# The operands of a second feed-forward layer: x on VectorE, two sums per round kept in DRAM, operands split four products ahead

## The chip, the cores and the metric

One core of a Trainium2 chip runs the whole program. The metric is the device time of one execution in microseconds (us). Engines are named as in the profile: PE is the matmul engine TensorE, PEld its weight loads, DVE is VectorE, ACT is ScalarE, POOL is GpSimd, SP is SyncE, whose queue issues nearly all transfers.

## What is computed

Pooled attention (4 batches, 8 heads, 576 tokens) gives a matrix x of 2304 tokens by 512. A gated layer of width 1536 follows, and then the layer in which the change lies (`_moe2_ref` of the reference, d_ff = 2048):

```python
h = x @ w_in
sp = np.where(h > 20.0, h, np.log1p(np.exp(np.minimum(h, 20.0))))
g = h * np.tanh(sp)
return (g @ w_out).astype(np.float32)
```

The nonlinearity is Mish. All inputs and outputs are float32.

## The kernel before

The 2304 tokens are worked in three **pairs** of two groups of 384 tokens (`NG = 384`, `p` = 0, 1, 2; "second pair" is p = 1, "last pair" is p = 2). Each float32 matmul is made of three matmuls of a rounded type: a tile is split into a high part (ACT casts it, L1197) and a low part (DVE subtracts the high part, L1201), and high*high, low*high and high*low are added up in PSUM.

Both products, x @ w_in and g @ w_out, are taken as 2x2 block products with seven block multiplications instead of eight (Winograd's form), in which sums of blocks are multiplied. So x, the weights and g are needed in sums, and those are split into high and low parts as well.

For the second and the last pair the work stands in two stages:

- **Rounds.** Eight rounds `i` = 0..7, each with seven products of x (`product(k)`, L122 to L124, 42 matmuls of 384 columns), one after the other on PE. DVE adds each product to a running sum (L1347), ACT applies Mish. A round leaves four blocks of g: `a`, `g2[2i]`, `g2[2i+1]` and `u`. From these two operands (`gu`, `gd`) go at once into the output accumulators `acc` (18 matmuls, in the next round). The weights of the next round come from DRAM in four transfers (`split_weights`, L1231).
- **Jobs.** Then 40 jobs of 9 matmuls of 256 columns each (`job`, L1289) add the other five output products: eight of kind 1 (operand `a_at[i]`), eight of kind 5 (operand S1 = `a_at[i]` + `g2[2i]`, L1496), eight of kind 6 (operand `g2[2i]`), eight of kind 7 (operand S3 = `g2[2i+1]` - `g2[2i]`, L1502), eight of kind 4 (operand `g2[2i+1]`). The order is written out: 1 x8, 5 x3, 6 x8, 5 x3, 7 x8, 5 x2, 4 x8; the last two run in the next pair's first round. Between jobs 2 and 4 stand the last round's two operands (18 matmuls to `acc`). The operand of job j+3 is split behind job j (`operand`), into one of four buffers `g`. DVE forms S1 in place behind the job of kind 1, and S3 behind the job of kind 6. The right-hand sides of the kinds 5, 6, 7 and 4 come from DRAM (`load_sum`, L1283), each into the place of one that is no longer used. `ob` is a pool of three buffers for output rows.

While the second pair's jobs run, the x of the last pair is made: `load_x2` (L146) brings four blocks for each half k of the depth, and `prep_x2_pool` makes 7 sums, each with a high part by ACT (L178) and a low part by POOL (L181), and 4 differences by POOL (L184). For the second pair the same is made by DVE in `prep_x2` (L157, L160), while the first pair's jobs run.

Every engine runs its instructions in the order in which they are written; SP too, so that a transfer that waits holds up all behind it.

Of the kernel before, what the change touches and what calls it, by code (L numbers as in the profile page):

```python
# [57 lines left out]
def tile_pooled_attention_moe_mish(  # L58
# [42 lines left out]
    w2od = [dram.tile([128, 512], F32, name=f"w2od{i}") for i in range(NF2)]  # L101
    wsd = [dram.tile([128, 2, 512], F32, name=f"wsd{i}") for i in range(NF)]
    wspd = [[dram.tile([128, 2, n], F32, name=f"wp{i}_{j}") for j, n in enumerate((512, 512, 512, 256))] for i in range(NFP)]
    td = [dram.tile([128, 4, 2, 256], F32, name=f"td{i}") for i in range(NFP)]

    def acc_tiles():
# [19 lines left out]
    with tc.manual_schedule():  # L126
# [42 lines left out]
                [lo(4, b21)],  # L169
            ]  # L170

        def prep_x2_pool(k, j):

            P, A = nc.gpsimd, nc.scalar
            b11, b12, b21, b22 = (st_t[r, c] for r, c in ((0, 0), (0, 1), (1, 0), (1, 1)))

            def hi(i, t):
                return lambda: A.copy(out=top[i, k][0], in_=t)  # L178

            def lo(i, t):  # L180
                return lambda: P.tensor_sub(out=top[i, k][1], in0=t, in1=f32(top[i, k][0]))  # L181

            def sub(out, a, b):
                return lambda: P.tensor_sub(out=out, in0=a, in1=b)  # L184

            return {
                j: [hi(1, b11), hi(3, b22), hi(2, b21), lo(1, b11), sub(b11, b12, b11), sub(b12, b22, b12)],
                j + 1: [lo(3, b22), sub(b22, b22, b11), lo(2, b21), sub(b21, b21, b22)],
                j + 5: [hi(5, b11)],
                j + 6: [hi(7, b12), lo(5, b11)],  # L190
                j + 7: [hi(6, b22), lo(7, b12)],
                j + 9: [hi(4, b21), lo(6, b22), lo(4, b21)],
            }

        def prep_w(ws, st):

# [975 lines left out]
        with ExitStack() as bctx:  # L1172
# [131 lines left out]
                        rhs = [w[:, b, half[h]] for b in range(2)]  # L1304
                        out_half(acc[t][0][:, half[h]], g, t, rhs, i + h == 0, i == NFP - 1)

            pend, after, keep = [], None, []
            g2 = {}
            for p in range(NPR):
                o = 2 * NG * p  # L1310
# [5 lines left out]
                for i in range(NFP):  # L1316
                    n = NFP * p + i
                    wt = w_sets[i % 2]
                    f1, f2 = 2 * i, 2 * i + 1
                    if p == 0:  # L1320
                        split_weights(i, True)
                        tt = load_rows_out(i)
                    if NFP <= n + 1 < NFP * NPR and i < NFP - 1:
                        split_weights((i + 1) % NFP, False)
                    if wino and 0 < i < 5:
                        for m in (2 * i - 2, 2 * i - 1):
                            load_sum(5, m)

                    a = a_at[i] if wino else a7
                    u = u0 if wino or i % 2 == 0 else a6  # L1330
                    if p == 0:
                        for f in (f1, f2):
                            g2[f] = late[f] if f in late else pb.tile([128, NG], F32, name=f"g2_{f}")

                    def product(k, *reads):

                        ps, home = bank(f"p{k}")
                        part, c0 = PART[k]
                        for kk in range(2):
                            xh, xl = top[k, kk]  # L1340
                            c = slice(c0 + 128 * kk, c0 + 128 * kk + 128)
                            mm3(ps[:, :NG], wt[part], c, xh, xl, kk == 0, kk == 1)
                        for out, in0 in reads:
                            if in0 is None:
                                nc.scalar.copy(out=out, in_=ps[:, :NG])
                            else:
                                nc.vector.tensor_add(out=out, in0=in0, in1=ps[:, :NG])  # L1347
                        banks.append(home)

                    product(1, (a, None))  # L1350
                    product(6, (u, a))
                    product(5, (v, u))
                    product(7, (g2[f2], v), (u, u))
                    nc.scalar.activation(out=g2[f2], in_=g2[f2], func=AF.Mish)  # L1354
                    if i == NFP - 1:
                        gs = {}
                        for f in range(2):
                            src = a_at[f] if wino else g2[f]
                            gs[f] = high(src, False)
                            low(src, gs[f])  # L1360
                        if wino:
                            g = gs[2] = w_sets[0][0][:, :, :NG]
                            A.copy(out=g[:, 0, :], in_=a_at[2])
                            low(a_at[2], g)
                    if p == 0 and i < NFP - 1:
                        run_all(prep_w(ws_of.pop(n + 1), w_sets[(i + 1) % 2]) if n else rows)
                    run_all([keep[:1]])
                    if n + 3 < NFP:
                        load_ws(n + 3)
                    run_all([pend])  # L1370
                    if after is not None:
                        after()
                    pend, after = [], None
                    if acc is None:
                        acc = [bank(f"acc{t}") for t in range(NTG)]
                    product(2, (a, a))
                    if wino:
                        A.activation(out=a, in_=a, func=AF.Mish)
                        product(3, (g2[f1], v))
                        A.activation(out=g2[f1], in_=g2[f1], func=AF.Mish)  # L1380
                        V.tensor_sub(out=v, in0=g2[f2], in1=a)
                        product(4, (u, u))
                        A.activation(out=u, in_=u, func=AF.Mish)
                        V.tensor_add(out=g2[f1], in0=g2[f1], in1=v)
                        V.tensor_sub(out=v, in0=u, in1=g2[f1])
                        gu, gd = high(u, False), high(v, False)
                        low(u, gu)
                        low(v, gd)
                        pend = [lambda i=i, acc=acc, gu=gu, gd=gd: out_pair(acc, i, gu, gd)]
# [56 lines left out]

                def operand(j):

                    if 2 < j <= last:
# [12 lines left out]

                more = {}
                if not final:
                    more = prep_x2_pool(0, 3)
# [10 lines left out]
                for j, (k, i) in enumerate(jobs[:-2]):  # L1476
# [7 lines left out]
                    if 8 <= j < 11 or 19 <= j < 22:  # L1484
                        t, h = (j - 8, 0) if j < 11 else (j - 19, 1)
                        x = ob[t][:, half[h]]
                        V.tensor_add(out=x, in0=x, in1=X[t][0][:, half[0]])
                        if h == 0:
                            leave(x, 128 * t, 0)
                    if j == 29:  # L1490
                        for t in range(NTG):
                            A.copy(out=c22[t], in_=X[t][0][:, half[0]])
                    if j < 2 or j > 3:
                        operand(j + 3)
                    if k == 1:
                        V.tensor_add(out=a_at[i], in0=a_at[i], in1=g2[2 * i])  # L1496
                        load_sum(6, i)
                    if k == 5:
                        load_sum(4, i)
                    if k == 6:  # L1500
                        load_sum(7, i)
                        V.tensor_sub(out=g2[2 * i], in0=g2[2 * i + 1], in1=g2[2 * i])  # L1502
                    if 4 <= j < 7:
                        t = j - 4
                        ob[t] = pb.tile([128, 512], F32, tag="ob", name="ob", bufs=3)
# [7 lines left out]
                        banks.append(Y[t][1])  # L1513
                    run_all([more.pop(j, [])])
                    if not final:
                        if j == 5:
                            split_weights(0, False)
                        if j == 17:
                            load_x2(p + 1, 1)
                            more = prep_x2_pool(1, 22)  # L1520
                if final:
                    for t in range(NTG):
                        for j in (last - 1, last):
# [49 lines left out]
```

## Time and profile before

| | us |
|---|---|
| three runs, lowest / median / highest | 869.18 / 869.37 / 870.87 |
| the profiled execution, its own time | 869.25 |
| its span, first to last instruction | 867.5 |
| PE busy / share of the span | 854.8 / 99% |
| DVE busy / share | 632.7 / 73% |
| ACT busy / share | 452.2 / 52% |
| POOL busy / share | 173.7 / 20% |

The table says which engine is filled over the whole span; a matmul's end is modelled, so a busy PE is not PE at its best rate. What a stage leaves unused is seen from the starts of matmuls: in undisturbed stretches they follow each other at a fixed distance.

### The profile page before, as it was taken

What the parts mean: (1) busy time and instruction counts of PE and PEld (TensorE: products, weight loads), DVE (VectorE), ACT (ScalarE), POOL (GpSimd) and SP (SyncE); (2) the same over time, 40 slices, a digit from 0 to 9 for tenths busy, and PEclk for the clock granted to TensorE, in tenths of its full rate; (3) what the DMA queues carried; (4) which work ended last, traced back from release to release, by engine and by line L of the source; (5) the groups of instructions that cost most, each with busy time, mean ns of one, the idle gap of its engine ahead of it and who ended that gap; (6) DMA issues with size and microseconds to landing.
All of it is one profiled execution on the core that took longest, in us unless ns stands there. A gap on an engine that the chain in (4) does not pass through costs nothing.

```text
span 867.5 us, 14376 instructions
## 1 busy us (share of the span) xinstructions
PE 854.8 (99%) x5044; PEld 782.1 (90%) x5044; DVE 632.7 (73%) x1160; ACT 452.2 (52%) x1083; POOL 173.7 (20%) x182
## 2 busy tenths in 40 slices
PE   8999999999999999999999999999999989999998
PEld 7878887888888888999999999998999979999998
DVE  6989764776675565878998877766666798667784
ACT  7655675555565554534545655555333455334454
POOL 3566430210210000001100045442000065000000
PEclk9999999999999999999999999999999999999999
DMA  9898527998788876256658789987577355777353
GB/s 344 305 315 266 176 79 241 283 274 252 243 263 265 226 222 218 97 201 229 237 198 294 271 297 336 325 307 251 195 258 255 115 198 168 245 244 225 125 189 100
DMA packets 113891, 202.30 MB, mean 233 GB/s; under 512 B 34588, under 2 KB 64284, under 8 KB 113820
## 3 DMA queue, kind: packets, MB, share of 16 engines
q1 hardware_dynamic: 112812, 199.40, 69.4%
q10 hardware_dynamic: 1008, 2.00, 0.7%
q8 instruction: 40, 0.66, 0.3%
q14 instruction: 31, 0.25, 0.1%
HBM read 141.44 MB, written 53.62 MB: 225 GB/s over the span
## 4 chain that ended last, share of the span: by engine, by line
PE 86%; DVE 5%; ACT 4%; DMA 2%; issue 1%; POOL 1%; SPq 0%; ACTq 0%; DVEq 0%
PE acc L1207 8%; PE x L1289 7%; PE p L124 7%; PE p L122 7%; PE p L123 7%; PE acc L122 4%; PE acc L123 4%; PE acc L124 4%; PE acc L1289 4%; PE q L123 3%; PE q L124 3%; PE q L122 3%; PE pv L593 3%; PE pv L594 3%; PE pv L597 3%; PE pg L593 3%
## 5 line engine op out<-in xcount | busy, mean ns | idle before, releaser
L122 PE MATMUL p<-top,w2s 128*128 128x384 f32 x216 | 72.4, 335 | 0.0
L124 PE MATMUL p<-top,w2s 128*128 128x384 f32 x216 | 72.4, 335 | 0.0
L123 PE MATMUL p<-top,w2s 128*128 128x384 f32 x216 | 72.4, 335 | 0.0
L1207 PE MATMUL acc<-w,g 128*128 128x512 f32 x288 | 67.1, 391 | 0.0
L1207 PEld LDWEIGHTS acc<-w,g 128*128 128x128 f32 x288 | 54.0, 188 | 10.9
L954 ACT CAST gh<-sg 128x512 fp32r<-128x512 f32 x36 | 22.3, 621 | 69.8 <-DVE sg L949 69.8
L122 PE MATMUL acc<-gh,wo 128*128 128x512 f32 x144 | 57.1, 397 | 0.0
L123 PE MATMUL acc<-gl,wo 128*128 128x512 f32 x144 | 56.4, 391 | 0.0
L124 PE MATMUL acc<-gh,wo 128*128 128x512 f32 x144 | 56.2, 390 | 0.0
L1201 DVE TENSOR_TENSOR g<-g,g 128x384 fp32r<-128x384 f32 x64 | 41.4, 662 | 19.0 <-ACT g L1197 18.7
L1197 ACT CAST g<-g 128x384 fp32r<-128x384 f32 x64 | 31.8, 512 | 30.4 <-PE x L1289 15.8
L456 ACT ACTIVATE e<-sc,mx 128x72 f32<-128x72 f32 x144 | 43.7, 333 | 3.1 <-DVE mx L444 3.0
L1085 POOL TENSOR_TENSOR g<-g,y 128x384 f32<-128x384 f32 x12 | 12.2, 1016 | 153.6 <-ACT g L1082 153.6
L122 PEld LDWEIGHTS p<-top,w2s 128*128 128x128 f32 x216 | 40.7, 188 | 0.3
L123 PEld LDWEIGHTS p<-top,w2s 128*128 128x128 f32 x216 | 40.7, 188 | 0.3
L124 PEld LDWEIGHTS p<-top,w2s 128*128 128x128 f32 x216 | 40.6, 188 | 0.0
L124 PE MATMUL p<-x1c,w2s 128*128 128x384 f32 x120 | 40.1, 335 | 0.0
L122 PE MATMUL p<-x1c,w2s 128*128 128x384 f32 x120 | 40.1, 334 | 0.0
L123 PE MATMUL p<-x1c,w2s 128*128 128x384 f32 x120 | 40.1, 334 | 0.0
L1289 PE MATMUL x<-w2s,g 128*128 128x256 f32 x288 | 38.4, 293 | 1.8 <-DVE g L1201 1.0
L1354 ACT ACTIVATE g<-g 128x384 f32<-128x384 f32 x24 | 12.6, 525 | 51.7 <-DVE g L1347 51.7
L1289 PEld LDWEIGHTS x<-w2s,g 128*128 128x128 f32 x288 | 36.7, 199 | 3.1 <-DVE g L1201 1.7
(324 smaller groups left out, 2538.0 us busy)
## 6 DMA issues: line engine op xcount, KB each, us to landing
w2s<-wp SPq DMA_DIRECT2D x48, 512.0 KB
wo<-wod SPq DMA_DIRECT2D x39, 512.0 KB
wp<-w2s SPq DMA_DIRECT2D x24, 512.0 KB
raw<-w2i SPq DMA_DIRECT2D x16, 512.0 KB
raw<-w2o SPq DMA_DIRECT2D x16, 512.0 KB
w<-td SPq DMA_DIRECT2D x32, 256.0 KB
w2s<-td SPq DMA_DIRECT2D x32, 256.0 KB
wr<-wv SPq DMA_DIRECT2D x12, 512.0 KB
```

The lines of the kernel that those rows point to most:

```text
L122: nc.tensor.matmul(ps, wt[:, 0, cols], xh, start=start, stop=False)
L123: nc.tensor.matmul(ps, wt[:, 0, cols], xl, start=False, stop=False)
L124: nc.tensor.matmul(ps, wt[:, 1, cols], xh, start=False, stop=stop)
L456: nc.scalar.activation(out=e_t[T][:, 4 * g + h, :], in_=s[:, h, :], func=AF.Exp, scale=-1.0, bias=mx_t[T][:, 4 * g + h, :], accum_out=sm_t ...
L593: nc.tensor.matmul(ps[:, c0:c1], w, xh[:, k, c0:c1], start=(k == 0), stop=False)
L594: nc.tensor.matmul(ps[:, c0:c1], w, xl[:, k, c0:c1], start=False, stop=False)
L597: nc.tensor.matmul(ps[:, c0:c1], w, xh[:, k, c0:c1], start=False, stop=(k == KD - 1))
L954: nc.scalar.copy(out=gh, in_=sg)
L1197: nc.scalar.copy(out=g[:, 0, :], in_=src)
L1201: nc.vector.tensor_sub(out=g[:, 1, :], in0=src, in1=f32(g[:, 0, :]))
L1207: nc.tensor.matmul(acc[t][0], g[:, a, c], w[:, b, :], start=(f == 0 and first), stop=(f == NF2 - 1 and last),)
L1289: nc.tensor.matmul(ps, g[:, a, c], rhs[b], start=start and a + b == 0, stop=stop and a == 1, skip_group_check=True)
```

## The change

1. The low parts and differences of the last pair's x move from POOL to DVE, spread over one job each (`prep_x2_slots` in the place of `prep_x2_pool`). The second half's blocks are loaded behind job 11 instead of job 17, and the weights of the last pair's first round behind job 23 instead of job 5.
2. In the rounds 0 to 5 of the second pair, S1 is formed as `g2[2i]` (before its last subtraction) + `g2[2i+1]`, and S3 one round later, each in a buffer of `ob`, and both are stored to DRAM (`sd`, 12 transfers of 192 KB). During the jobs they are loaded again over `a_at[m]` and `g2[2m]` (12 transfers). The sums of rounds 6 and 7 are formed among the jobs 13 to 16. In the last pair all sums stay with their jobs.
3. In both pairs the operands of jobs 0 to 4 are split before the jobs begin, the first three into the place of round 6's weights, and from then on an operand is split four jobs ahead. The additions of `ob` stand together behind jobs 8 and 19.

```diff
-        def prep_x2_pool(k, j):
+        def prep_x2_slots(k, j):
...
-                return lambda: P.tensor_sub(out=out, in0=a, in1=b)
-
-            return {
-                j: [hi(1, b11), hi(3, b22), hi(2, b21), lo(1, b11), sub(b11, b12, b11), sub(b12, b22, b12)],
-                j + 1: [lo(3, b22), sub(b22, b22, b11), lo(2, b21), sub(b21, b21, b22)],
...
+                return lambda: V.tensor_sub(out=out, in0=a, in1=b)
+
+            parts = [
+                [hi(1, b11)],
+                [lo(1, b11), hi(3, b22)],
+                [sub(b11, b12, b11)],
+                [sub(b12, b22, b12), hi(2, b21)],
+                [lo(3, b22), hi(5, b11)],
+                [sub(b22, b22, b11), hi(7, b12)],
+                [lo(2, b21)],
+                [sub(b21, b21, b22), hi(6, b22)],
+                [lo(5, b11)],
+                [lo(7, b12), hi(4, b21)],
+                [lo(6, b22)],
+                [lo(4, b21)],
+            ]
+            return {j + m: part for m, part in enumerate(parts)}
...
                     product(7, (g2[f2], v), (u, u))
                     nc.scalar.activation(out=g2[f2], in_=g2[f2], func=AF.Mish)
+                    run_all([late_sum])
+                    run_all([spill])
...
-                        V.tensor_add(out=g2[f1], in0=g2[f1], in1=v)
+                        if kept:
+                            sums = [pb.tile([128, 512], F32, tag="ob", name="sk", bufs=3)[:, :NG] for _ in range(2)]
+                            V.tensor_add(out=sums[0], in0=g2[f1], in1=g2[f2])
+                            V.tensor_sub(out=g2[f1], in0=sums[0], in1=a)
+                            spill = [
+                                lambda m=m, i=i, x=x: nc.sync.dma_start(out=sd[i][m], in_=x) for m, x in enumerate(sums)
+                            ]
+                        else:
+                            V.tensor_add(out=g2[f1], in0=g2[f1], in1=v)
...
+                        if kept:
+                            late_sum = [
+                                lambda x=sums[1], f1=f1, f2=f2: V.tensor_sub(out=x, in0=g2[f2], in1=g2[f1])
+                            ]
...
-                    if j < 2 or j > 3:
-                        operand(j + 3)
-                    if k == 1:
-                        V.tensor_add(out=a_at[i], in0=a_at[i], in1=g2[2 * i])
+                    if j > 2:
+                        operand(j + 4)
+                    if final:
+                        if k == 1:
+                            V.tensor_add(out=a_at[i], in0=a_at[i], in1=g2[2 * i])
+                        if k == 6:
+                            V.tensor_sub(out=g2[2 * i], in0=g2[2 * i + 1], in1=g2[2 * i])
+                    else:
+                        for m in {0: (0, 1, 2), 8: (3,), 9: (4,), 10: (5,)}.get(j, ()):
+                            nc.sync.dma_start(out=a_at[m], in_=sd[m][0])
+                        if 12 <= j < 18:
+                            nc.sync.dma_start(out=g2[2 * (j - 12)], in_=sd[j - 12][1])
...
-                        if j == 5:
+                        if j == 23:
                             split_weights(0, False)
-                        if j == 17:
+                        if j == 11:
                             load_x2(p + 1, 1)
-                            more = prep_x2_pool(1, 22)
+                            more = prep_x2_slots(1, 17)
```

How the change moves instructions is shown at three places. First VectorE among the second pair's jobs 5 to 10. `g` is an operand's low part, `aw`, `a6`, `a7` hold `a_at`, `st` a block of x and `top` its high and low parts, `ob` with `x0` to `x2` is an addition of output rows. Before:

```order
L1496 TENSOR_TENSOR a6_5248<-a6_5248,g2_12_5242 128x384
L1201 TENSOR_TENSOR g_7338<-aw_6422,g_7338 128x384
L1496 TENSOR_TENSOR a7_5249<-a7_5249,g2_14_5244 128x384
L1487 TENSOR_TENSOR ob_7287<-ob_7287,x0_7190 128x256
L1201 TENSOR_TENSOR g_7357<-g2_0_5257,g_7357 128x384
L1487 TENSOR_TENSOR ob_7307<-ob_7307,x1_7191 128x256
```

Now:

```order
L1209 TENSOR_TENSOR g_7345<-aw_6437,g_7345 128x384
L185 TENSOR_TENSOR st_7042<-st_7042,st_7039 128x384
L1209 TENSOR_TENSOR g_7362<-aw_6438,g_7362 128x384
L182 TENSOR_TENSOR top3_3565<-st_7042,top2_3564 128x384
L1209 TENSOR_TENSOR g_7378<-g2_0_5273,g_7378 128x384
L185 TENSOR_TENSOR st_7042<-st_7042 128x384
L1520 TENSOR_TENSOR ob_7332<-ob_7332,x0_7240 128x256
L1520 TENSOR_TENSOR ob_7349<-ob_7349,x1_7241 128x256
L1520 TENSOR_TENSOR ob_7366<-ob_7366,x2_7242 128x256
L1209 TENSOR_TENSOR g_7399<-g2_2_5362,g_7399 128x384
```

The operand's low part alternates with an operation of x instead of a sum, and the three output additions stand together.

Second, VectorE at the end of round 4 and up to the pending operands of the second pair's round 5 (`p2` to `p7` are products, `sk` the buffers of the kept sums), now:

```order
L1355 TENSOR_TENSOR u_5262<-u_5262,p4_6922 128x384
L1402 TENSOR_TENSOR sk_6931<-g2_8_5254,g2_9_5255 128x384
L1403 TENSOR_TENSOR g2_8_5254<-sk_6931,aw_6439 128x384
L1409 TENSOR_TENSOR v_5263<-u_5262,g2_8_5254 128x384
L1209 TENSOR_TENSOR g_6936<-u_5262,g_6936 128x384
L1209 TENSOR_TENSOR g_6938<-v_5263,g_6938 128x384
L1355 TENSOR_TENSOR u_5262<-aw_6439,p6_6954 128x384
L1355 TENSOR_TENSOR v_5263<-u_5262,p5_6962 128x384
L1355 TENSOR_TENSOR g2_11_5257<-v_5263,p7_6970 128x384
L1355 TENSOR_TENSOR u_5262<-u_5262,p7_6970 128x384
L1415 TENSOR_TENSOR sk_6932<-g2_9_5255,g2_8_5254 128x384
```

The two operations with L1402 and L1403 stand where there was one subtraction ahead of the addition of `p4` and one addition behind it; L1415 is new in the round.

Third, SP's queue from job 11 on: `w2s` with `td` is a right-hand side of kind 7, `st` a block of x, `g2` with `sd` an S3 that comes back. Now:

```order
L1291 DMA w2s_4957<-td0_167 128x512
L147 DMA st_7452<-x2d1_67 128x384 x2
L147 DMA st_7455<-x2d3_69 128x384 x2
L1488 DMA out<-ob_7366 128x256
L1537 DMA g2_0_5273<-sd0_1_152 128x384
L1291 DMA w2s_4957<-td1_168 128x512
L1537 DMA g2_2_5362<-sd1_1_154 128x384
L1291 DMA w2s_4958<-td2_169 128x512
```

Before, the right-hand sides of kind 7 stood one behind the other here, and the blocks of x behind the seventh of them.

## Rows read from the trace of the kernel before

**Rows 1.** The page's first part: busy us, share of the span, instructions by engine.

```profile
PE 854.8 (99%) x5044; PEld 782.1 (90%) x5044; DVE 632.7 (73%) x1160; ACT 452.2 (52%) x1083; POOL 173.7 (20%) x182
```

**Rows 2.** Timeline of PE, second pair's jobs: start, length, instructions, idle before, releaser.

```profile
690.30 2.31 PE L1289 MATMUL x<-w,g 128*128 128x256 f32 x18
...
701.08 0.40 PE L1289 MATMUL y<-w,g 128*128 128x256 f32 x2
...
707.10 1.09 PE L1289 MATMUL y<-w,g 128*128 128x256 f32 x7 [1.23 <-DVE g L1201]
...
710.79 9.66 PE L1289 MATMUL x<-w2s,g 128*128 128x256 f32 x66 [0.18 <-DVE ob L1487]
...
736.20 7.26 PE L1289 MATMUL x<-w,g 128*128 128x256 f32 x54
743.30 0.34 PE L122 MATMUL p<-top,w2s 128*128 128x384 f32 x1
743.47 0.34 PE L123 MATMUL p<-top,w2s 128*128 128x384 f32 x1
```

**Rows 3.** Timeline of PE, last pair's jobs.

```profile
818.77 2.31 PE L1289 MATMUL x<-w,g 128*128 128x256 f32 x18
...
855.48 8.80 PE L1289 MATMUL x<-w,g 128*128 128x256 f32 x72
```

**Rows 4.** Windows: stretch, its length, busy us (instructions) by engine, PEclk, DMA share, GB/s.

```profile
708.00:712.00 4.00, 2.82 (x15) 2.12 (x14) 4.00 (x9) 0.93 (x2) 1.19 (x1) 0.89 0.42 110
712.00:716.00 4.00, 4.00 (x26) 4.00 (x26) 2.53 (x6) 1.54 (x4) 1.43 (x1) 0.68 0.90 284
```

**Rows 5.** Timeline of DVE, second pair's jobs.

```profile
692.92 0.56 DVE L1201 TENSOR_TENSOR g<-v,g 128x384 fp32r<-128x384 f32 x1
...
694.80 1.02 DVE L1496 TENSOR_TENSOR aw<-aw,g 128x384 f32<-128x384 f32 x2
...
700.56 1.37 DVE L1201 TENSOR_TENSOR g<-aw,g 128x384 fp32r<-128x384 f32 x1
...
727.43 5.20 DVE L1201 TENSOR_TENSOR g<-g,g 128x384 fp32r<-128x384 f32 x4 [2.60 <-ACT g L1197]
...
739.46 0.41 DVE L1511 TENSOR_TENSOR ob<-ob,y 128x256 f32<-128x256 f32 x1
739.79 0.41 DVE L1511 TENSOR_TENSOR u<-u,y 128x256 f32<-128x256 f32 x1
```

**Rows 6.** Timeline of POOL, second pair's jobs.

```profile
700.18 1.33 POOL L181 TENSOR_TENSOR top<-st,top 128x384 fp32r<-128x384 f32 x1
...
733.46 5.20 POOL L181 TENSOR_TENSOR x1c<-st,x1c 128x384 fp32r<-128x384 f32 x4
```

**Rows 7.** Windows, as rows 4: the second pair's jobs.

```profile
690.00:743.00 53.00, 48.30 (x361) 45.50 (x360) 47.46 (x72) 28.58 (x61) 27.69 (x22) 0.97 0.56 185
```

**Rows 8.** Timeline of DVE, first pair's jobs, where DVE makes x.

```profile
609.11 0.55 DVE L1201 TENSOR_TENSOR g<-g,g 128x384 fp32r<-128x384 f32 x1
609.58 0.55 DVE L157 TENSOR_TENSOR x1c<-st,x1c 128x384 fp32r<-128x384 f32 x1
```

**Rows 9.** Windows, as rows 4: the second pair's rounds, two stretches of other transfers.

```profile
620.00:680.00 60.00, 60.00 (x380) 59.81 (x378) 39.06 (x74) 22.62 (x45) 0.00 (x0) 1.00 0.73 246
722.00:725.00 3.00, 3.00 (x28) 3.00 (x27) 2.12 (x5) 1.55 (x4) 0.00 (x0) 1.00 0.96 314
664.00:668.00 4.00, 4.00 (x30) 4.00 (x29) 3.13 (x6) 1.42 (x3) 0.00 (x0) 1.00 0.97 376
```

**Rows 10.** Timeline of SP and ACT: blocks of x, and the weights of a round.

```profile
719.82 1.81 SPq L146 DMA_DIRECT2D st<-x2d  x4
...
724.56 0.51 ACT L178 CAST top<-st 128x384 fp32r<-128x384 f32 x1 [0.32 <-DMA st<-x2d]
...
631.81 4.84 SPq L1231 DMA_DIRECT2D w2s<-wp  x4
```

More of the change, by code (lines that the diff above doesn't have):

```diff
@@ L103, in tile_pooled_attention_moe_mish @@
     wspd = [[dram.tile([128, 2, n], F32, name=f"wp{i}_{j}") for j, n in enumerate((512, 512, 512, 256))] for i in range(NFP)]
+    sd = [[dram.tile([128, NG], F32, name=f"sd{i}_{j}") for j in range(2)] for i in range(NFP)]
     td = [dram.tile([128, 4, 2, 256], F32, name=f"td{i}") for i in range(NFP)]
@@ L170, in prep_x2 @@
             ]
-        def prep_x2_pool(k, j):
-            P, A = nc.gpsimd, nc.scalar
+        def prep_x2_slots(k, j):
+            V, A = nc.vector, nc.scalar
             b11, b12, b21, b22 = (st_t[r, c] for r, c in ((0, 0), (0, 1), (1, 0), (1, 1)))
@@ L180, in lo @@
             def lo(i, t):
-                return lambda: P.tensor_sub(out=top[i, k][1], in0=t, in1=f32(top[i, k][0]))
+                return lambda: V.tensor_sub(out=top[i, k][1], in0=t, in1=f32(top[i, k][0]))
             def sub(out, a, b):
-                return lambda: P.tensor_sub(out=out, in0=a, in1=b)
-            return {
-                j: [hi(1, b11), hi(3, b22), hi(2, b21), lo(1, b11), sub(b11, b12, b11), sub(b12, b22, b12)],
-                j + 1: [lo(3, b22), sub(b22, b22, b11), lo(2, b21), sub(b21, b21, b22)],
[L189 to L193, printed above, removed]
+                return lambda: V.tensor_sub(out=out, in0=a, in1=b)
[14 more added lines that the diff above has]
+            return {j + m: part for m, part in enumerate(parts)}
         def prep_w(ws, st):
@@ L1305, in out_pair @@
                         out_half(acc[t][0][:, half[h]], g, t, rhs, i + h == 0, i == NFP - 1)
-            pend, after, keep = [], None, []
+            pend, after, keep, spill, late_sum = [], None, [], [], []
             g2 = {}
@@ L1350, in tile_pooled_attention_moe_mish @@
                     product(1, (a, None))
+                    if i == NFP - 1 and wino:
+                        gs = {}
+                        for f in range(3):
+                            gs[f] = w_sets[0][f][:, :, :NG]
+                            A.copy(out=gs[f][:, 0, :], in_=a_at[f])
                     product(6, (u, a))
@@ L1354, in tile_pooled_attention_moe_mish @@
                     nc.scalar.activation(out=g2[f2], in_=g2[f2], func=AF.Mish)
-                    if i == NFP - 1:
+                    run_all([late_sum])
+                    run_all([spill])
+                    late_sum, spill = [], []
+                    if i == NFP - 1 and wino:
+                        for f in range(3):
+                            low(a_at[f], gs[f])
+                    elif i == NFP - 1:
                         gs = {}
                         for f in range(2):
[L1358 to L1364, printed above, removed]
+                            gs[f] = high(g2[f], False)
+                            low(g2[f], gs[f])
                     if p == 0 and i < NFP - 1:
@@ L1380, in tile_pooled_attention_moe_mish @@
                         A.activation(out=g2[f1], in_=g2[f1], func=AF.Mish)
-                        V.tensor_sub(out=v, in0=g2[f2], in1=a)
+                        kept = not final and i < NFP - 2
+                        if not kept:
+                            V.tensor_sub(out=v, in0=g2[f2], in1=a)
                         product(4, (u, u))
                         A.activation(out=u, in_=u, func=AF.Mish)
-                        V.tensor_add(out=g2[f1], in0=g2[f1], in1=v)
+                        if kept:
[7 more added lines that the diff above has]
+                            V.tensor_add(out=g2[f1], in0=g2[f1], in1=v)
                         V.tensor_sub(out=v, in0=u, in1=g2[f1])
@@ L1388, in tile_pooled_attention_moe_mish @@
                         low(v, gd)
+                        if kept:
+                            late_sum = [
+                                lambda x=sums[1], f1=f1, f2=f2: V.tensor_sub(out=x, in0=g2[f2], in1=g2[f1])
+                            ]
+                        if i == NFP - 1:
+                            for f in range(3, 5):
+                                gs[f] = high(a_at[f], False)
+                                low(a_at[f], gs[f])
                         pend = [lambda i=i, acc=acc, gu=gu, gd=gd: out_pair(acc, i, gu, gd)]
@@ L1447, in operand @@
                 def operand(j):
-                    if 2 < j <= last:
+                    if 4 < j <= last:
                         k, i = jobs[j]
@@ L1464, in tile_pooled_attention_moe_mish @@
                 if not final:
-                    more = prep_x2_pool(0, 3)
+                    more = prep_x2_slots(0, 0)
                 ob, Y = {}, []
@@ L1483, in tile_pooled_attention_moe_mish @@
                         job(Y if k == 5 else X, j, t)
[L1484 to L1489, printed above, removed]
+                    if j in (8, 19):
+                        h = (8, 19).index(j)
+                        for t in range(NTG):
+                            x = ob[t][:, half[h]]
+                            V.tensor_add(out=x, in0=x, in1=X[t][0][:, half[0]])
+                    if 10 <= j < 13:
+                        leave(ob[j - 10][:, half[0]], 128 * (j - 10), 0)
                     if j == 29:
@@ L1492, in tile_pooled_attention_moe_mish @@
                             A.copy(out=c22[t], in_=X[t][0][:, half[0]])
-                    if j < 2 or j > 3:
-                        operand(j + 3)
+                    if j > 2:
[10 more added lines that the diff above has]
+                            nc.sync.dma_start(out=g2[2 * (j - 12)], in_=sd[j - 12][1])
+                        if 13 <= j < 15:
+                            V.tensor_add(out=a_at[j - 7], in0=a_at[j - 7], in1=g2[2 * (j - 7)])
+                        if 15 <= j < 17:
+                            m = j - 9
+                            V.tensor_sub(out=g2[2 * m], in0=g2[2 * m + 1], in1=g2[2 * m])
                     if k == 1:
-                        V.tensor_add(out=a_at[i], in0=a_at[i], in1=g2[2 * i])
                         load_sum(6, i)
@@ L1501, in tile_pooled_attention_moe_mish @@
                         load_sum(7, i)
-                        V.tensor_sub(out=g2[2 * i], in0=g2[2 * i + 1], in1=g2[2 * i])
                     if 4 <= j < 7:
```

## The prediction

> **What bounds the kernel now.** I read the page first, then PE's timeline, then the timelines of DVE and POOL where PE waits. PE is busy for 99% of the span [rows 1], so at most about 1% is to be had, and only where PE's matmuls fall apart. PE's undisturbed rate is in the last pair's jobs: 72 matmuls of 256 columns in 8.80 us, the last one 0.28 long, give (8.80 - 0.28) / 71 = 0.120 us each [rows 3]. A job of 9 is thus 1.08 us. From the first job to the start of the 72 are 32 jobs and 18 other matmuls, 306 in all: 306 x 0.120 = 36.7 us, and 855.48 - 818.77 = 36.71 is what it took. The last pair's jobs lose nothing.
>
> The second pair's do. From the first job at 690.30 to the next pair's first product at 743.30 stand 38 jobs and the same 18 matmuls, 360 in all: 43.2 us of work, 53.0 us of time [rows 2]. **9.8 us are lost**: 9.2 of them before 736.20 (45.90 against 36.71), 0.6 behind. Where PE stands idle, it waits for DVE's low part of an operand (L1201), as with 1.23 us at 707.10. Some 1.6 us of it are slow matmuls, not waits: from 710.79 a run of 66 took 9.66 us instead of 66 x 0.120 + 0.16 = 8.1, and the granted clock there is 0.89 and then 0.68 [rows 4]. Of the two levels, 2.4 and 1.2 GHz, PE thus ran a part of this stretch at the lower, after being busy only 2.82 of the 4 us ahead of it. These 1.6 us follow from the waits and should go with them.
>
> Why DVE is late is seen in its own timeline beside POOL's. Two sums in a row take 1.02 us at 694.80, so a distance of 1.02 - 0.55 = 0.47. While POOL works on x (as at 700.18, and from 733.46 to 738.7, [rows 6]) the same instructions take 1.37 us, and the four at 727.43 stand (5.20 - 1.35) / 3 = 1.28 apart [rows 5]. POOL's own four at 733.46 fill 5.20 as well. With a split and a sum per job DVE then needs 2.6 us per 1.08 us of PE.
>
> **The change part by part.**
>
> *x from POOL to DVE.* POOL loses 22 instructions, 27.7 us [rows 7], and has nothing left in this stretch. DVE gains 22. Their price on DVE is known: in the first pair's jobs DVE makes x alone, in turn with operands, at 0.55 us each and 0.47 apart [rows 8]. That is 22 x 0.47 = 10.3 us.
>
> *Sums.* 12 of the 16 leave the jobs (-12 x 0.47 = 5.6 us). In each of six rounds DVE gets one instruction more, 0.47 us in the 9.3 us of a round (42 matmuls at 0.17 and 18 at 0.12, [rows 2, 3]), where it is busy 39.06 of 60 us [rows 9]. I cost it at nothing. The two instructions behind product 4 make `gd` about 0.4 us later; it is not used before the four products of the next round (4 x 6 x 0.17 = 4.1 us, 0.17 being the distance of the two products at 743.30) are done, so it stays covered.
>
> *DVE's account in the jobs.* With 33 splits left, 22 operations of x and 4 sums at 0.47, and 12 output additions at 0.33 (739.79 - 739.46, [rows 5]): 59 x 0.47 + 12 x 0.33 = 31.7 us, in about 40 us of jobs. Job by job: jobs 5 to 11 carry a split and an x, 0.94 us of 1.08. Job 8 has three additions more, 1.0 us, and there DVE falls behind. An operand split four ahead can be cast when job j frees its buffer, so three jobs, 3.24 us, are left for cast (0.5), subtraction (0.55) and queue. Walking DVE's order with these distances, from its last split of the rounds at 692.92 [rows 5] and with PE's job 8 at 701.08 [rows 2], I find the operand of job 12 ready some 0.5 us before it is due, the tightest place, and DVE level again by job 16. PE does not stop there. ACT has one cast per job, half a cast of x, and three copies in jobs 4 to 6; it runs 0.7 us late at job 6 and is level at job 9.
>
> *New transfers.* The stores, 2 x 192 KB per round, go behind the weights in SP's queue. The weights for a round are issued when the round two ahead has done its last products, as at 631.81, so a whole round of 9 us before they are due, and take 1.8 MB at 314 GB/s, 6 us; the stores add 0.39 MB / 314 GB/s = 1.25 us [rows 9, 10]. The DMA share of the rounds rises from 0.73 to about 0.85. Cost nothing. The first three reloads of S1 wait only for the splits of round 7, and run before the crowd.
>
> *The crowded place* is job 11 and what follows: four blocks of x, then in each job one S3 (192 KB) and one right-hand side (256 KB). SP issues the last blocks of x only when DVE has read `b21`, by my walk near 708; S3 of pair 0 goes out near 709.7 and is to be cast when job 18 ends, 701.08 + 11 x 1.08 = 713.0. Each pair is 448 KB, at the 314 GB/s of 1.5 KB rows 1.46 us, 0.38 more than a job: what starts 1.1 us early is 0.8 late at the sixth. A late cast has 1.6 us before PE feels it. So 0 is the near bound. The far bound is the slowest landing that I saw in this stretch: the blocks issued from 719.82 let ACT go only at 724.56, 4.7 us later [rows 10]. With 4.7 us S3 lands at 714.4, 1.4 us late; PE loses 0 to 1 us. I take 0.3. The Trainium skill, page DMA: Bandwidth & Descriptors, section Anatomy of one DMA, fits a transfer with 2.0 us plus its bytes at 436 GB/s. By that rule a reload is there 2.5 us after its issue, nothing is late, and the sum below would come out 0.3 us lower; the fit is for transfers from GpSimd's queue, and no run here shows it for SP's.
>
> *Weights of the last pair's first round* are issued behind job 21 or so instead of among the first jobs, and have 16 jobs, 17 us, for 1.8 MB: covered. *The last pair* splits four ahead too; it loses nothing now, so nothing is to be had, and with POOL silent nothing to lose.
>
> **Sum.** 869.25 (the profiled execution; the median of the runs is 869.37, 0.1 above) - 9.8 + 0.3 = **859.7 us**. Against the median that is -9.7 us, 1.1%. A difference under 0.2% (1.7 us) could not be told from none.
>
> **The rivals.**
>
> *The reloads are late (2 in 10).* The S3 loads queue behind x and PE takes the waits over from DVE. For it: this stretch carries 0.8 MB of x, 1.2 of S3, 2.1 of right-hand sides and 0.1 of output in the time of eight jobs, 4.2 MB in 8.6 us or nearly 490 GB/s, where the fastest row shown is 376 GB/s [rows 9]. Against it: needs are staggered as well, and the buffers give 1.6 us. Price: if the transfers run only at 246 GB/s, the mean of the rounds, a pair takes 1.87 us, and the sixth S3 is 5 x (1.87 - 1.08) = 4 us behind; with the 4.7 us landing, 1.4 + 4 - 1.6 = 3.8 us of waits. If the granted clock falls again, some 1.6 more: 861 to 865, likeliest 863.
>
> *The losses are not DVE's (3 in 100).* If PE waited for something that the change leaves as it is, the time stays at 869.3. Against it: the last pair runs the same jobs, with splits and sums on DVE but no x on POOL, at 0.120 us throughout [rows 3].
>
> *DVE gets slower, not faster (3 in 100).* If DVE's 1.28 came from something other than POOL, the 22 new instructions would cost as much: from 693.5, the end of that last split [rows 5], 59 x 1.28 + 4 = 79.5 us, so the stage would end near 773 instead of 743.3: 899 us. It decides at a mean distance of (743.3 - 693.5 - 4) / 59 = 0.78 us: above it the kernel is slower than now. Against it stand the 0.47 of the first pair [rows 8] with POOL still.
>
> **How the numbers follow.** The forecast has 74 in 100 and a range of its own of 859.1 (all 9.8 us, no new wait, 0.3 for the runs' scatter) to 860.8 (1 us of late loads). The late reloads have 20. The range that holds 8 in 10 takes in the part of these up to 862.5: **859.1 to 862.5**. Faster by over 0.2%: 74 + 20 = 94; within 0.2%: 3; slower: 3.
>
> **What would show it.** Right: from 690.3 the jobs stand in one unbroken run and the last pair's first product starts near 733.6; DVE's subtractions of x are 0.55 long; POOL has no instruction behind the first pair; PEclk is 1.00 throughout; the last pair's jobs still take 36.7 us to the run of 72. Wrong in a term: idle of PE before jobs 22 to 28, released by DVE's L1209, with ACT's casts ended by a DMA `g2<-sd` or `st<-x2d` (late reloads); PE idle near job 12 (DVE's additions); PE idle inside the second pair's rounds (the stores or the new sums). The whole is wrong if DVE's instructions stay at 1.3 us with POOL idle.

## The result, and the profile after

| | before | after |
|---|---|---|
| median of 4 runs, us | 869.9 | 860.53 |
| lowest to highest | 869.18 to 870.87 | 860.21 to 860.67 |
| the profiled execution, its own time / its span | 869.25 / 867.5 | 860.67 / 858.9 |

The ratio is 0.9891 (95% interval 0.9874 to 0.9908): the changed kernel is about 9.4 us faster. The forecast was 859.7 us, in a range of 859.1 to 862.5. (The kernel before was timed once more beside it, at 870.43 us, so its median is now that of four runs.)

The page's first part of the changed kernel, against [rows 1]:

```profile
PE 850.8 (99%) x5044; PEld 780.6 (91%) x5044; DVE 625.6 (73%) x1176; ACT 452.2 (53%) x1083; POOL 146.8 (17%) x160
```

POOL has lost its 22 instructions and the 27 us of [rows 7]. DVE has 16 more and is busy 7 us less: its sums and low parts beside POOL had become longer, and are so no more. The shares say nothing of the gain; PE is at 99% in both.

PE's timeline of the changed kernel, second pair's jobs, against [rows 2] (start, length, instructions, idle before and releaser, where there was an idle that the view shows):

```profile
690.77 3.39 PE L1297 MATMUL x<-w,w2s 128*128 128x256 f32 x27
...
701.56 3.40 PE L1297 MATMUL y<-w,g 128*128 128x256 f32 x27
704.80 8.80 PE L1297 MATMUL x<-w2s,g 128*128 128x256 f32 x72
713.44 3.40 PE L1297 MATMUL y<-w,g 128*128 128x256 f32 x27
716.96 9.28 PE L1297 MATMUL x<-w2s,g 128*128 128x256 f32 x72
...
728.23 6.64 PE L1297 MATMUL x<-w,g 128*128 128x256 f32 x54
734.71 0.34 PE L123 MATMUL p<-top,w2s 128*128 128x384 f32 x1
```

From the first job to the last pair's first product it is 734.71 - 690.77 = 43.94 us, where it was 53.00. The 360 matmuls need 43.2 at 0.120 us each, so 9.8 us of loss have become 0.74. The first 72 of kind 6 take 8.80 us, as long as the undisturbed 72 of [rows 3]. All that is left of the loss stands behind 713.44: 27 matmuls from there end at 713.44 + 3.24 = 716.68, the next starts at 716.96 (0.28 lost), and its 72 take 9.28 instead of 8.80 (0.48 lost).

DVE's timeline of the changed kernel, where in [rows 5] an instruction took 1.3 us:

```profile
702.17 0.55 DVE L182 TENSOR_TENSOR top<-st,top 128x384 fp32r<-128x384 f32 x1
702.63 0.55 DVE L1209 TENSOR_TENSOR g<-g,g 128x384 fp32r<-128x384 f32 x1
703.10 0.55 DVE L185 TENSOR_TENSOR st<-st 128x384 f32<-128x384 f32 x1
703.57 1.07 DVE L1520 TENSOR_TENSOR ob<-ob,x 128x256 f32<-128x256 f32 x3
704.57 0.55 DVE L1209 TENSOR_TENSOR g<-g,g 128x384 fp32r<-128x384 f32 x1
```

Low parts of x, of operands and differences are all 0.55 long and 0.47 apart. The last line is the operand of job 12, ready at 705.12; job 11 ends near 705.9.

Windows of the changed kernel: the rounds, the jobs, and two stretches of the jobs (columns as in [rows 4]):

```profile
620.00:680.00 60.00, 60.00 (x379) 59.72 (x378) 41.94 (x80) 22.26 (x44) 0.00 (x0) 1.00 0.87 282
691.00:734.00 43.00, 42.80 (x355) 42.41 (x354) 37.57 (x81) 27.72 (x61) 0.00 (x0) 1.00 0.81 271
712.00:716.00 4.00, 4.00 (x36) 4.00 (x35) 2.09 (x5) 1.85 (x4) 0.00 (x0) 1.00 1.03 338
716.00:720.00 4.00, 3.88 (x33) 3.71 (x32) 4.00 (x11) 2.37 (x5) 0.00 (x0) 1.00 0.89 279
```

The granted clock is 1.00 in all of them: the lower level of [rows 4], and its 1.6 us, went with the waits. In the rounds DVE's 39.06 us and the DMA share of 0.73 [rows 9] have become 41.94 and 0.87, with no idle time on PE.

What is late now is read from four timelines of the changed kernel: SP, ACT, DVE and PE's weight loads (PEld). `g<-sd` is an S3 that comes back.

```profile
706.87 2.39 SPq L147 DMA_DIRECT2D st<-x2d  x4
...
709.98 0.32 SPq L1537 DMA_DIRECT2D g<-sd  x1
...
715.07 0.38 SPq L1537 DMA_DIRECT2D g<-sd  x1
```

```profile
714.95 0.51 ACT L1205 CAST g<-g 128x384 fp32r<-128x384 f32 x1 [1.47 <-DMA g<-sd]
...
720.68 0.51 ACT L1205 CAST g<-g 128x384 fp32r<-128x384 f32 x1 [1.32 <-DMA g<-sd]
```

```profile
715.50 0.56 DVE L1209 TENSOR_TENSOR g<-g,g 128x384 fp32r<-128x384 f32 x1 [1.83 <-ACT g L1205]
715.98 0.55 DVE L182 TENSOR_TENSOR top<-st,top 128x384 fp32r<-128x384 f32 x1
716.44 1.08 DVE L1520 TENSOR_TENSOR ob<-ob,x 128x256 f32<-128x256 f32 x3
...
721.23 0.56 DVE L1209 TENSOR_TENSOR g<-g,g 128x384 fp32r<-128x384 f32 x1 [0.90 <-ACT g L1205]
```

```profile
721.84 4.19 PEld L1297 LDWEIGHTS x<-w2s,g 128*128 128x128 f32 x34 [0.29 <-DVE g L1209]
```

S3 of round 0 (the prediction calls it S3 of pair 0) is issued at 709.98 and lets ACT go at 714.95, 5.0 us later. DVE waits 1.83 us for that cast. Its low part itself is for job 22 and would be in time; but behind it in DVE's queue stand an operation of x and the three output additions (L1520), which begin at 716.44 and free the accumulators that job 22 writes. So here a late transfer reaches PE through instructions that have nothing to do with it. The other 0.48 us come the direct way. S3 of round 4 is issued at 715.07 and lets ACT go at 720.68, 5.6 us later; its low part starts at 721.23 and ends at 721.79, and the weight load of job 26 that reads it (721.84) waits for it. The matmuls there start 0.36 and 0.23 us apart instead of 0.12, which is 0.35 of the 0.48 us.

**Where the 8.6 us between the two profiled executions lie:** 869.25 - 9.80 + 0.74 = 860.19; the measured one is 860.67. Some 0.4 of the rest is at the very start, where q arrives a little later in this execution; before and after:

```profile
9.11 1.25 PE L433 MATMUL sc<-kb,q 128*128 128x144 f32 x8 [0.30 <-DMA q<-qt]
```

```profile
9.55 1.25 PE L441 MATMUL sc<-kb,q 128*128 128x144 f32 x8 [0.71 <-DMA q<-qt]
```

Nothing of the change acts there, and in the runs below the second pair's first job starts anywhere between 690.4 and 691.5 us. Differences of some 0.5 us between single executions are therefore read from the jobs' own stretch, not from the total. "Loss" below is always the time from the second pair's first job to the last pair's first product, less 43.2 us.

### The profile page after: what moved, and what is told of

The parts are those of the page before. It is cut to its first block, busy times and chain, and to the rows that moved or that the text cites. A ratio compares the mean times of both kernels' runs of the same rounds, so it can differ in the third digit from the quotient of the medians.

```text
span 858.9 us, 14424 instructions
## 1 busy us (share of the span) xinstructions
PE 850.8 (99%) x5044; PEld 780.6 (91%) x5044; DVE 625.6 (73%) x1176; ACT 452.2 (53%) x1083; POOL 146.8 (17%) x160
## 4 chain that ended last, share of the span: by engine, by line
PE 90%; ACT 4%; DMA 3%; DVE 2%; issue 1%; POOL 0%; SPq 0%; ACTq 0%
PE acc L1215 8%; PE p L123 7%; PE p L125 7%; PE p L124 7%; PE x L1297 7%; PE acc L123 5%; PE acc L124 4%; PE acc L125 4%; PE acc L1297 4%; PE q L123 3%; PE q L125 3%; PE q L124 3%; PE pv L601 3%; PE pv L602 3%; PE pv L605 3%; PE pg L601 3%
## 5 line engine op out<-in xcount | busy, mean ns | idle before, releaser
L1209 DVE TENSOR_TENSOR g<-g,g 128x384 fp32r<-128x384 f32 x64 | 35.8, 567 | 17.2 <-ACT g L1205 16.8
L1297 PE MATMUL acc<-w,g 128*128 128x256 f32 x288 | 37.3, 283 | 0.0
L957 DVE SCALAR_TENSOR_TENSOR sg<-sg,pv 128x512 f32<-128x512 f32 x34 | 23.1, 680 | 18.9 <-PE pv L605 18.9
```

Source lines behind the costliest of these rows:

```text
L957: nc.vector.scalar_tensor_tensor(out=sg, in0=sg, scalar=1.0, in1=pv[:, :n], op0=ALU.add, op1=ALU.mult)
L1209: nc.vector.tensor_sub(out=g[:, 1, :], in0=src, in1=f32(g[:, 0, :]))
L1297: nc.tensor.matmul(ps, g[:, a, c], rhs[b], start=start and a + b == 0, stop=stop and a == 1, skip_group_check=True)
```

## The experiments

Theory: DVE was the late engine, because its instructions take longer while POOL subtracts, and because it had too much to do in the jobs; what is left is reloads of S3 that land late. Rivals: it is the number of DVE's instructions alone; it is the distance at which operands are split; it is POOL's being busy in any way.

**The parts apart.** Four kernels, all timed beside the same runs of the kernel before (median 869.91).

*Only x moved.* The kernel before with `prep_x2_slots`; the sums stay in the jobs, operands are split three ahead, the output additions stay apart.

```diff
-    more = prep_x2_pool(0, 3)
+    more = prep_x2_slots(0, 0)
...
-    if j == 5:
+    if j == 23:
         split_weights(0, False)
-    if j == 17:
+    if j == 11:
         load_x2(p + 1, 1)
-        more = prep_x2_pool(1, 22)
+        more = prep_x2_slots(1, 17)
```

> The kernel before with x on VectorE alone (the spread of one step per job, the loads and the weights moved as in the change); sums stay among the jobs, operands three ahead. Theory 1 (VectorE is late because its instructions take 1.3 us while GpSimd works): VectorE's operations are 0.55 us long throughout; jobs 1 to 7 carry split, x and sum, 3 x 0.47 = 1.41 us for 1.08 us of PE, some 2 to 3 us behind plus 1 us of output additions, of which the buffers hide 2 to 3: PE loses 1 to 2.5 us of its former 9.8, so 861 to 863 us. Theory 2 (VectorE is late because it has too many instructions, GpSimd beside it does not matter): 22 more of them make it worse, 875 us or more.

Measured: 863.67 us (862.78 to 864.01), ratio 0.9925 (0.9905 to 0.9945); loss 3.3 us. DVE does more instructions in the jobs than before, all 0.55 long, and the kernel is 6.2 us faster: that it is their number alone is excluded. The time is 0.7 above the expected range. PE's timeline shows what stayed:

```profile
707.12 0.62 PE L1296 MATMUL x<-w2s,g 128*128 128x256 f32 x3 [0.42 <-DVE ob L1494]
...
721.38 8.18 PE L1296 MATMUL x<-w2s,g 128*128 128x256 f32 x66 [0.65 <-DVE ob L1494]
```

PE waits for output additions that stand behind sums, splits and x in DVE's queue: 2.2 us of the loss lie at jobs 11 to 18, 1.1 at jobs 22 to 29, and none elsewhere. DVE's timeline has the first and the last of the three additions ahead of job 11:

```profile
705.39 0.41 DVE L1494 TENSOR_TENSOR ob<-ob,x 128x256 f32<-128x256 f32 x1
...
707.92 0.41 DVE L1494 TENSOR_TENSOR ob<-ob,x 128x256 f32<-128x256 f32 x1
```

*All but x moved.* The changed kernel, with the low parts and differences of x back on POOL, in the new places.

```diff
-            V, A = nc.vector, nc.scalar
+            V, A = nc.gpsimd, nc.scalar
```

> The changed kernel with the low parts and differences of x back on GpSimd, at their new places; sums kept in DRAM, operands four ahead. Theory 1: 22 operations of GpSimd fill some 28 us, in which VectorE gets one instruction per 1.28 us where PE asks for one per 1.08; PE loses 0.2 us in each of some 22 jobs and the output additions, 3 to 6 us: 863 to 866 us. Theory 2: VectorE has only the 33 splits, 4 sums and 12 additions, 21 us in 40 us of jobs; PE loses no more than in the changed kernel, 860 to 861 us.

Measured: 863.13 us (861.6 to 864.61), ratio 0.992 (0.9897 to 0.9943); loss 3.45 us. DVE's timeline of this kernel, beside POOL's subtractions:

```profile
718.35 9.09 DVE L1209 TENSOR_TENSOR g<-g,g 128x384 fp32r<-128x384 f32 x7
```

Seven operands are (9.09 - 1.3) / 6 = 1.3 us apart, and PE loses in steps of about 0.2 us in the jobs beside them. The two parts don't add up: x alone brings 6.2 us, all without x 6.8, together 9.4. Each frees so much of DVE's time in the jobs that little is left for the other to bring.

*Sums back among the jobs.* The changed kernel with nothing kept in DRAM.

```diff
-                        kept = not final and i < NFP - 2
+                        kept = False
...
-                    if final:
+                    if True:
```

> The changed kernel without the kept sums: S1 and S3 are formed among the jobs of the second pair, as in the last pair; no stores and reloads. Theory 1: the same account as for x alone, but the first five operands are split ahead: PE loses 0.5 to 2 us in jobs 5 to 12, and nothing later, as the late reloads are gone: 860 to 862 us. Theory 2: 12 sums more on VectorE cost at least their 12 x 0.47 = 5.6 us: 866 us or more.

Measured: 862.08 us (861.31 to 862.29), ratio 0.9906 (0.9882 to 0.993); 0.1 above the expected range; loss 1.2 us, of which some 0.8 at job 11 and 0.35 at job 22. I had expected nothing at job 22, as there are no reloads here. There is: the three output additions stand at 718.01 in DVE's queue, now behind sums. The kept sums are worth some 0.5 to 0.8 us of loss. The additions ahead of job 11 stand together here:

```profile
705.77 1.08 DVE L1520 TENSOR_TENSOR ob<-ob,x 128x256 f32<-128x256 f32 x3
```

*Three ahead.* The changed kernel, with only three operands split before the jobs.

```diff
-                            for f in range(3, 5):
-                                gs[f] = high(a_at[f], False)
-                                low(a_at[f], gs[f])
...
-                    if j > 2:
-                        operand(j + 4)
+                    if j < 2 or j > 3:
+                        operand(j + 3)
```

> The changed kernel with operands split three jobs ahead, and only the first three split before the jobs. Theory 1: the four buffers are freed at the same moments, so ACT casts at the same times; PE loses at most 1 us more than in the changed kernel, 860 to 861.5 us. Rival (the fourth operand ahead is what ends the waits): PE's waits of 0.5 to 1.2 us per job come back in jobs 5 to 12, 865 us or more.

Measured: 861.11 us (860.45 to 861.48), ratio 0.9896 (0.9876 to 0.9916); loss 0.71 us, as in the changed kernel. With x and the sums out of the way, the fourth operand ahead is worth nothing that can be measured. What divides the first kernel (3.3) from the third (1.2) is therefore more likely the grouping of the output additions, which this kernel has as well. Those two edits were not tried apart, but the lines above fit it: with the first job at the same time (691.50 and 691.47), the first addition starts at 705.39 and 705.77, while the last starts at 707.92 where the additions stand apart and near 706.4 where they stand together (0.33 us from one to the next).

**What it is in POOL's work that holds DVE up.** Two kernels add work to POOL beside DVE's 11 operations on x's first half, in the changed kernel; its results are read by nobody. In one POOL subtracts a tile of 128x384, in the other it fills one of 128x1024 behind a subtraction of one column.

```diff
+                    nc.gpsimd.tensor_sub(out=w[:, 0, :NG], in0=x, in1=x)
```

> The changed kernel with 11 subtractions of 128x384 added on GpSimd in jobs 1 to 11, beside the first half of x; they read a tile of x and write a place that nobody reads. Theory 1: for some 14 us VectorE's instructions take 1.3 us; two per job are asked for, so it falls some 8 us behind, of which buffers hide 3: PE loses 4 to 7 us, with a fall of the granted clock 1 to 2 more, 864 to 869 us. Theory 2 (GpSimd beside it does not matter): VectorE stays at 0.55 us, 860.5 us.

```diff
+                    nc.gpsimd.tensor_sub(out=w[:, 0, :1], in0=x[:, :1], in1=x[:, :1])
+                    nc.gpsimd.memset(f32(w).rearrange("p a n -> p (a n)"), 0.0)
```

> As the run with 11 subtractions added on GpSimd, but 11 fills of 128x1024 in their place (about 1.1 us each, some 12 us in all), which write and read nothing; a subtraction of one column ahead of each keeps them in their jobs. If any work of GpSimd holds VectorE up: the same 5 us of PE's waits as with the subtractions, 864 to 867 us. If only work that reads does, as the Trainium skill has it (page SBUF: State Buffer, section SBUF: two separate sides): VectorE's operations stay at 0.55 us and the time at 860.5 to 861.2 us.

Measured: with subtractions 865.58 us (864.02 to 865.88), ratio 0.9944 (0.9927 to 0.9961), loss 5.6 us, of which 3.7 lie in the jobs up to 18 and 1.9 at job 22, where ACT waits 3.06 us for an S3 that SP issues at 714.37 instead of 709.98; with fills 860.44 us (860.23 to 860.77), ratio 0.9889 (0.9875 to 0.9904), as the changed kernel. Timelines of POOL and DVE with the subtractions:

```profile
694.70 9.70 POOL L184 TENSOR_TENSOR w2s<-top 128x384 fp32r<-128x384 f32 x9 [93.02 <-ACT top L179]
```

```profile
698.13 1.18 DVE L1222 TENSOR_TENSOR g<-a,g 128x384 fp32r<-128x384 f32 x1
699.23 1.18 DVE L195 TENSOR_TENSOR st<-st 128x384 f32<-128x384 f32 x1
...
704.73 0.55 DVE L195 TENSOR_TENSOR st<-st 128x384 f32<-128x384 f32 x1
```

Windows of the same kernel (columns as in [rows 4]):

```profile
698.00:702.00 4.00, 2.31 (x19) 2.11 (x18) 4.00 (x5) 2.74 (x7) 3.77 (x4) 1.00 0.16 60
706.00:710.00 4.00, 2.81 (x22) 2.43 (x21) 4.00 (x8) 1.96 (x5) 1.72 (x2) 1.00 0.75 218
```

POOL and DVE with the fills:

```profile
702.28 0.22 POOL L184 TENSOR_TENSOR w2s<-top 128x1 fp32r<-128x1 f32 x1
702.56 0.95 POOL L185 MEMSET w2s<- 128x1024 f32 x1
```

```profile
702.83 0.55 DVE L1223 TENSOR_TENSOR g<-g,g 128x384 fp32r<-128x384 f32 x1
703.30 0.55 DVE L196 TENSOR_TENSOR st<-st 128x384 f32<-128x384 f32 x1
```

Beside subtractions DVE's instructions are 1.10 us apart, and 0.55 long again as soon as POOL pauses; beside a fill of 0.95 us two of them run in their usual 0.47. So it is not that POOL is busy, nor that it writes. What a subtraction does beyond a fill is to read SBUF and to compute; these two runs don't part the two. The Trainium skill, page SBUF — State Buffer, section SBUF: two separate sides, says that a DVE instruction with two inputs in SBUF is held up by a GpSimd instruction that reads SBUF, and by no other, and that the one that starts first keeps the shared ports to its end. The traces agree: 1.10 us beside reads, 0.47 beside fills.

**The late reloads.** Three kernels move only transfers (and in the last the second half of x with them). Each is timed beside a repeat of the changed kernel on the same chip; the first repeat gave 860.91 us (860.7 to 861.05), ratio 0.9897 (0.988 to 0.9913), loss 0.43; the second 861.2 us (860.93 to 862.13), ratio 0.9901 (0.9885 to 0.9918), loss 0.6.

> The changed kernel unaltered, beside the next kernels on the same chip: 860.5 us again, 0.7 us of PE's waits in jobs 22 to 29.

> The changed kernel unaltered once more, beside the run with S3 early on the same chip: 860.5 to 860.9 us, with 0.4 to 0.8 us of PE's waits in jobs 22 to 29.

*S3 one job later.*

```diff
-                        if 12 <= j < 18:
-                            nc.sync.dma_start(out=g2[2 * (j - 12)], in_=sd[j - 12][1])
+                        if 13 <= j < 19:
+                            nc.sync.dma_start(out=g2[2 * (j - 13)], in_=sd[j - 13][1])
```

> The changed kernel with each reload of S3 issued one job later. Theory (late reloads of S3): ACT's casts for jobs 22 on come up to 1.1 us later and PE waits 0.7 to 2 us more, 861.2 to 862.5 us. Rival (VectorE's additions): no difference, 860.5 us.

Measured: 861.77 us (860.97 to 862.8), ratio 0.9907 (0.9888 to 0.9927); loss 1.44 us, 1.4 of it at job 22. ACT's and PE's timelines:

```profile
715.68 0.51 ACT L1205 CAST g<-g 128x384 fp32r<-128x384 f32 x1 [2.58 <-DMA g<-sd]
```

```profile
717.69 8.86 PE L1297 MATMUL x<-w2s,g 128*128 128x256 f32 x72 [1.24 <-ACT g L1205]
```

As expected, PE feels the reloads. The profile names a cast as what PE waited for; DVE's timeline shows the output additions again as the last step:

```profile
717.17 1.07 DVE L1520 TENSOR_TENSOR ob<-ob,x 128x256 f32<-128x256 f32 x3
```

The first of them, 0.41 long, ends at 717.58, and job 22 starts at 717.69.

*The last three S1 reloads earlier*, at job 5 instead of 8 to 10.

```diff
-  {0: (0, 1, 2), 8: (3,), 9: (4,), 10: (5,)}
+  {0: (0, 1, 2), 5: (3, 4, 5)}
```

> The changed kernel with the reloads of S1 of the rounds 3 to 5 behind job 5 instead of jobs 8 to 10, where the DMA engines are idle: 0.59 MB, 1.8 us at 314 GB/s, less in the crowded stretch. Theory (the last 0.7 us are late reloads of S3): S3 lands 1 to 1.8 us sooner, PE's waits in jobs 22 to 29 go from 0.7 to 0 to 0.2 us, 859.8 to 860.1 us. Rival (these waits come from VectorE's output additions behind job 19): they stay, 860.5 us.

Measured: 860.03 us (859.92 to 860.72), ratio 0.9888 (0.9871 to 0.9906), 0.9 under the repeat beside it. Half a miss: the wait at job 22 is gone, but 0.5 us of loss remains in the profiled execution (its slowest), no less than the 0.43 of the repeat, so the gain shows in the other three times alone. The loss is now in the run of 72 from job 22 on, where ACT still waits for the second S3:

```profile
717.25 0.51 ACT L1205 CAST g<-g 128x384 fp32r<-128x384 f32 x1 [1.95 <-DMA g<-sd]
```

*And S3 three jobs earlier*, on top of the last edit, with x's second half two jobs later.

```diff
-                        if 12 <= j < 18:
-                            nc.sync.dma_start(out=g2[2 * (j - 12)], in_=sd[j - 12][1])
+                        if 9 <= j < 15:
+                            nc.sync.dma_start(out=g2[2 * (j - 9)], in_=sd[j - 9][1])
...
-                            more = prep_x2_slots(1, 17)
+                            more = prep_x2_slots(1, 19)
```

> The changed kernel with S1 of the rounds 3 to 5 loaded behind job 5, S3 loaded behind jobs 9 to 14 instead of 12 to 17, and the second half of x spread from job 19 on instead of 17. Theory (the last waits are late reloads and the queue of VectorE behind them): each S3 has some 3 us more, no cast waits for a transfer, PE loses 0 to 0.2 us in the jobs, 859.6 to 860.2 us. Rival (what is left is VectorE's number of operations around job 19): 0.3 us or more stay, 860.4 to 860.8 us.

Measured: 859.83 us (859.65 to 860.44), ratio 0.9883 (0.9869 to 0.9898), the fastest of all: 1.4 us under the repeat of the changed kernel beside it, with no overlap of their runs. The loss is 0. PE's and ACT's timelines:

```profile
713.18 3.40 PE L1297 MATMUL y<-w,g 128*128 128x256 f32 x27
716.42 8.80 PE L1297 MATMUL x<-w2s,g 128*128 128x256 f32 x72
```

```profile
713.38 0.51 ACT L1205 CAST g<-g 128x384 fp32r<-128x384 f32 x1 [0.57 <-PE x L1297]
```

ACT's cast of the first S3 now waits for PE to free its buffer, not for a transfer, and no instruction in these jobs waits for a transfer any more. At 0.120 us per matmul PE has nothing left to gain in this stage. Moving x two jobs on also took an operation of x from in front of the output additions, so this run alone does not part the reloads from DVE's work at job 19; that the reloads alone move PE's wait is shown by the run with S3 one job later.

## Why the prediction was right, and where a size was off

- **The 9.8 us that PE lost, and their cause:** right. All of it was in the second pair's jobs, and 9.1 us of it went. The 1.28 us of DVE's instructions were the doing of POOL's subtractions: 1.10 apart beside added subtractions, 0.47 beside fills and without either; that it is the reading rests on the page named above. The rivals "losses not DVE's" and "DVE gets slower" are out.
- **DVE's account at 0.47 each:** right. Job 12's operand, named as the tightest place, came 0.8 us ahead (0.5 forecast). What the account did not say is that either half of the change, x alone or everything but x, would have brought most of the gain (6.2 and 6.8 of 9.4 us).
- **The 1.6 us at the lower clock follow from the waits:** they went with them; the granted clock is 1.00 throughout the jobs. But not every wait of this size has that price: in the run with added subtractions PE is busy only 2.31 us from 698 to 702 and 2.81 us from 706 to 710, and the granted clock stays at 1.00 up to 728.
- **Stores and sums in the rounds at nothing:** right. The DMA share went to 0.87 (0.85 forecast), and PE has no idle there.
- **The crowded place** is the term that was mis-sized. Its mechanism was right: S3 of round 0 was issued at 709.98 (709.7 forecast) and landed in 5.0 us (4.7 taken as the slowest). PE lost 0.74 us, in repeats 0.43 and 0.6, inside the 0 to 1 that was given, but over the 0.3 that I chose. Two steps of the term failed. "A late cast has 1.6 us before PE feels it" is the allowance of the cast's own operand; job 22 needs the output additions too, which stand behind that operand's low part in DVE's queue. Its cast came 1.5 us late (713.44 to 714.95), inside the 1.6, and PE lost 0.28 us. And the far bound set the slowest landing against the first S3 alone, though the term had each S3 fall 0.38 us further behind: by its own numbers the sixth would have cost 1.4 + 5 x 0.38 - 1.6 = 1.7 us, not 1. Measured, S3 of round 4 took 5.6 us and its cast came some 2.6 us late (job 22 ends near 718.1), from which come most of the other 0.48 us. That the loss stayed under 1 us owes something to luck.
- **The sum:** 859.7 + 0.44 (the loss above the 0.3) + 0.44 (the start of the program, nothing of the change) = 860.6, against 860.67 of the profiled execution.

Still open is the grouping of the output additions, which was not tried by itself: that it divides the run with only x moved from the run with the sums back in the jobs rests on two traces.

## What to carry to other kernels

Where an engine's instructions have two lengths, look at what another engine does at that time: taking work off that other engine can pay even when the late engine has to do it itself (6.2 us here, with 22 instructions more on DVE). The allowance for a late input is that of its own consumer and of whatever stands behind that consumer in the queue, whichever is smaller; and where inputs come in a row, the last of them counts, not the first. When a change moves work into transfers, place them by the job in which the place becomes free and not by the one that needs them: with S3 three jobs earlier, S1 earlier too and half of x two jobs later, the last 0.7 us were gone.

## What the runs showed of the hardware that was not expected

- A POOL fill of 128x1024 (0.95 us) beside DVE costs DVE nothing (0.47 us apart), while a POOL subtraction of 128x384 brings it to 1.10.
- A reload of 192 KB took 5.0 us from its issue to the cast that needed it (709.98 to 714.95), and a later one 5.6 us (715.07 to 720.68), in stretches with a DMA share of 1.03 and 0.89. By the Trainium skill, page DMA: Bandwidth & Descriptors, section Anatomy of one DMA, 2.0 us plus the bytes at 436 GB/s would be, as an estimate, 2.5 us; the fit is for a transfer from GpSimd's queue, and this trace, with SP's queue and nearly full DMA engines, shows twice that.
